# O summed behind the second chunk of V transposes, O and dq packed by ScalarE: decode attention, forward and backward, on one core

## The chip, the cores and the metric

The kernel runs on one core of a Trainium2 chip. The metric is the device time in microseconds (us), the median of several executions. A ratio is the mean time of one kernel's fast runs over the mean of the other's from the same rounds, which is not quite the ratio of the medians quoted beside it.

## The reference

```python
# q, grad_out: [1, 32, 1, 128]; k, v: [1, 32, 8192, 128]; all bfloat16
scores = einsum('bhqd,bhkd->bhqk', q, k) * 128 ** -0.5
attn = softmax(scores)
out_0 = einsum('bhqk,bhkd->bhqd', attn, v)          # O
# out_1, out_2, out_3 = dq, dk, dv by the vector-Jacobian product with grad_out
```

For one query row a head, dk and dv are outer products (ds times q, p times dO), as large as K and V. The kernel reads 134 MB and writes 134 MB.

## The kernel before

Each head loads K and V (2 MB each), and stores dk and dv (2 MB each, in two halves of 1 MB). TensorE transposes V in four chunks, computes the scores of V (dO·V) from them, and sums O and dq over 64 tiles each with one weight load and one matmul of one column per tile. VectorE makes dk and dv. All transfers are issued in order from one queue.

```python
    def v_transposes(h, c):                       # 8 fp32 transposes, one ScalarE copy
        T_ps = psT.tile([P, CH // 2, P], F32, tag="T", name="T_ps")      # two buffers
        for i in range(CH // 2):
            nc.tensor.transpose(T_ps[:, i, :], words[:, m * P:(m + 1) * P], ident_f[:])
        nc.scalar.copy(X[:], T_ps[:])
    def v_scores(h, c):                           # 16 weight loads, 16 matmuls of 2 columns
        ...
    def contract(Xt, rep, out_col, first=0, last=NT):   # a sum: 64 weight loads, 64 matmuls
        for n in range(first, last):
            nc.tensor.matmul(out_col, lhsT=Xt[:, n, :], rhs=rep[:, n, 0:1],
                             start=(n == 0), stop=(n == NT - 1), skip_group_check=True)
    for h in range(H + 1):
        ...  # transposes of K on VectorE, scores of K; dk and dq of the head before; p
        v_transposes(h, 0)
        contract(Vt[h], x["p"], x["m"][:, 2:3])                     # the sum of O
        nc.scalar.copy(o_all[:, h:h + 1], x["m"][:, 2:3])
        v_transposes(h, 1)
        nc.tensor.matmul(x["m"][:, 1:2], lhsT=do_f[...], rhs=o_all[:, h:h + 1], ...)  # dO.O
        v_scores(h, 0)
        v_transposes(h, 2)
        v_scores(h, 1)
        v_transposes(h, 3)
        v_scores(h, 2)
        v_scores(h, 3)
        ...  # dv, its stores, the load of V of head h + 2
    # then, in no fixed order: pack O and dq with VectorE, transpose, store (8 KB each)
```

## Time and profile before

| | before |
|---|---|
| median of 3 runs | 656.67 us (656.61 to 656.91) |
| profiled span | 656.6 us, of a run that took 658.36 us |
| busy: TensorE matmul, VectorE, ScalarE | 79%, 78%, 28% |
| main transfer queue, share of 16 DMA engines | 97.5% |

The share of the transfer queue is an average over 16 engines. Near 100% it says that bytes bound the kernel, but an average cannot show one engine that is slower than the rest, and that engine ends the run. Two means were needed beside the views: the completion records (each transfer counts a semaphore up by 16, and the time of each count is in the trace) and the packet records (start, length and size of each packet, without the engine's number).

### The profile page before, as it was taken

Reading aid. Unit: us, or ns where it says so; the run is one execution under the profiler, and the core shown is the slowest. Engines: PE = TensorE matmul, PEld = TensorE weight load, DVE = VectorE, ACT = ScalarE, POOL = GpSimd, SP = SyncE. Lnnn points to the kernel's source line nnn. Section 1 sums busy time; section 2 is a strip of 40 time slices with the busy share of each in tenths; the row PEclk is TensorE's granted clock in tenths of the full one; section 3 lists DMA queues with packets and bytes.
Section 4 is the critical chain, followed back from the end, with each engine's and each line's share of the span. In section 5 each row is a group of like instructions: output and inputs, shape, how many; then the busy total and the mean of one; then the engine's idle time right before and its main releaser. Section 6 shows DMA issues by size and latency. Waiting matters only on the chain.

```text
span 656.6 us, 21096 instructions
## 1 busy us (share of the span) xinstructions
PE 520.1 (79%) x9705; PEld 485.8 (74%) x9705; DVE 513.8 (78%) x664; ACT 182.2 (28%) x321; POOL 0.7 (0%) x6
## 2 busy tenths in 40 slices
PE   2889788798888777788777887787877888777881
PEld 1888788688888667787777877787866778777881
DVE  5789789788897978778877779777787777887753
ACT  0332223223333122332222322223322233222330
POOL 0000000000000000000000000000000000000000
PEclk9955556656565666655556556666556555555555
DMA  8999999999999999999999999999999999999883
GB/s 334 408 389 428 424 422 430 420 423 430 424 424 428 425 428 423 428 424 427 428 424 426 428 424 425 428 428 423 428 425 424 431 421 426 419 418 412 374 339 149
DMA packets 29368, 269.82 MB, mean 411 GB/s; under 512 B 3424, under 2 KB 3424, under 8 KB 5472
## 3 DMA queue, kind: packets, MB, share of 16 engines
q1 hardware_dynamic: 29280, 268.48, 97.5%
q8 instruction: 76, 1.25, 0.7%
q14 instruction: 12, 0.10, 0.0%
HBM read 134.23 MB, written 134.23 MB: 409 GB/s over the span
## 4 chain that ended last, share of the span: by engine, by line
DMA 63%; PE 23%; DVE 8%; ACT 2%; issue 1%; SPq 0%; ACTq 0%; DVEq 0%
DMA Kt<-in_k_dram 35%; DMA out_dram<-G_dv 29%; PE T_ps L180 10%; DVE XK_sb L142 6%; PE s_ps L154 3%; PE dp_ps L197 2%; PE m_ps L197 2%; PE dp_ps L192 2%; ACT XT_sb L182 1%; PE m_ps L265 1%; PE m_ps L278 1%; DVE G_dk L207 1%; ACT e L277 1%; ACT qd L223 1%; PE s_ps L170 1%
## 5 line engine op out<-in xcount | busy, mean ns | idle before, releaser
L180 PE MATMUL T_ps<-ident_f,Vt 128*128 128x128 f32 x1024 | 237.8, 410 | 0.0
L180 PEld LDWEIGHTS T_ps<-ident_f,Vt 128*128 128x128 f32 x1024 | 198.8, 222 | 0.0
L142 DVE STREAM_TRANSPOSE XK_sb<-Kt 128x1024 f32<-128x1024 f32 x128 | 148.1, 1213 | 63.8 <-DMA Kt<-in_k_dram 63.7
L182 ACT COPY XT_sb<-T_ps 128x1024 f32<-128x1024 f32 x128 | 129.6, 1012 | 160.2 <-PE T_ps L180 160.2
L207 DVE TENSOR_TENSOR G_dv<-p_rep,qd 128x2048 bf16<-128x2048 bf16 x128 | 148.2, 1220 | 14.0 <-DMA out_dram<-G_dv 10.7
L207 DVE TENSOR_TENSOR G_dk<-ds_rep,qd 128x2048 bf16<-128x2048 bf16 x128 | 155.7, 1218 | 1.1
L192 PEld LDWEIGHTS <-XT_sb 128*128 128x128 bf16 x2048 | 77.5, 107 | 30.2 <-ACT XT_sb L182 27.1
L154 PE MATMUL s_ps<-q_blk,XK_sb 128*128 128x4 bf16 x2048 | 59.3, 168 | 44.4 <-DVE pdt L228 41.6
L192 PE MATMUL dp_ps<-do_blk,XT_sb 128*128 128x2 bf16 x2048 | 73.8, 166 | 24.3 <-ACT XT_sb L182 24.3
L154 PEld LDWEIGHTS <-XK_sb 128*128 128x128 bf16 x2048 | 56.8, 103 | 46.3 <-DVE pdt L228 43.4
L197 PE MATMUL dp_ps<-ds_rep,Kt 128*128 128x1 bf16 x2048 | 64.4, 165 | 2.8 <-issue 2.3
L197 PEld LDWEIGHTS <-Kt 128*128 128x128 bf16 x2048 | 59.8, 104 | 8.3 <-issue 8.3
L197 PEld LDWEIGHTS <-Vt 128*128 128x128 bf16 x2048 | 62.6, 105 | 2.0
L197 PE MATMUL m_ps<-p_rep,Vt 128*128 128x1 bf16 x2048 | 60.5, 166 | 0.0
L238 ACT COPY dq_all<-dp_ps 128x1 f32<-128x1 f32 x32 | 5.1, 159 | 191.2 <-PE dp_ps L197 191.2
L278 PEld LDWEIGHTS m_ps<-rs,ones_f 128*128 128x128 f32 x64 | 16.0, 311 | 48.6 <-ACT e L277 48.6
L278 PE MATMUL m_ps<-rs,ones_f 128*128 128x1 f32 x64 | 18.7, 362 | 39.2 <-ACT e L277 39.2
L265 PE MATMUL m_ps<-diag,ones_f 128*128 128x128 f32 x64 | 25.6, 500 | 2.3 <-issue 1.7
L230 DVE SCALAR_TENSOR_TENSOR ds_rep<-dp_ps,pdt,p_s 128x256 bf16<-128x256 f32 x32 | 15.5, 484 | 15.1 <-PE dp_ps L192 12.8
L274 DVE TENSOR_REDUCE nbias<-m_ps 128x1 f32<-128x128 f32 x32 | 9.3, 292 | 20.7 <-ACT qd L223 20.7
L287 ACT ACTIVATE p_rep<-e,rinv 128x256 bf16<-128x256 f32 x32 | 16.2, 508 | 30.3 <-DVE rinv L285 30.3
L223 ACT CAST qd<-m_ps 128x256 bf16<-128x256 f32 x32 | 11.9, 372 | 45.2 <-PE m_ps L219 45.2
(44 smaller groups left out, 161.5 us busy)
## 6 DMA issues: line engine op xcount, KB each, us to landing
Kt<-in_k_dram SPq DMA_DIRECT2D x31, 2048.0 KB, 27.7
Vt<-in_v_dram SPq DMA_DIRECT2D x31, 2048.0 KB, 27.4
out_dram<-G_dv SPq DMA_DIRECT2D x62, 1024.0 KB, 25.3
out_dram<-G_dk SPq DMA_DIRECT2D x62, 1024.0 KB, 25.3
Kt<-in_k_dram SPq DMA_DIRECT2D x4, 512.0 KB, 5.1
Vt<-in_v_dram SPq DMA_DIRECT2D x4, 512.0 KB, 8.2
out_dram<-G_dv SPq DMA_DIRECT2D x4, 512.0 KB, 13.2
out_dram<-G_dk SPq DMA_DIRECT2D x4, 512.0 KB, 9.7
```

Of the source, the lines that this page charges most:

```text
L142: nc.vector.transpose(XK[h][:, :, :, u, :], slots(Kt[h], u, NCH).rearrange("p g d -> p (g d)").bitcast(F32).rearrange("p (g w j) -> p g w ...
L154: nc.tensor.matmul(out[:, g, :], lhsT=cols[:, g, c // 2, c % 2], rhs=q_blk[:, h, c, :], start=(c == 0), stop=(c == 2 * NB - 1), skip_group ...
L180: nc.tensor.transpose(T_ps[:, i, :], words[:, m * P:(m + 1) * P], ident_f[:])
L182: nc.scalar.copy(X[:], T_ps[:])
L192: nc.tensor.matmul(st[h]["dp"][:, n:n + 2], lhsT=X[:, i, e2, :], rhs=do_blk[:, h, e2, :], start=(e2 == 0), stop=(e2 == 1), skip_group_chec ...
L197: nc.tensor.matmul(out_col, lhsT=Xt[:, n, :], rhs=rep[:, n, 0:1], start=(n == 0), stop=(n == NT - 1), skip_group_check=True)
L207: nc.vector.tensor_tensor(slots(G, r, 4).rearrange("p n (a b) -> p n a b", b=R), slots(rep, r, 4).unsqueeze(2).to_broadcast([P, Q, D // R, ...
L223: nc.scalar.copy(x["qd"][:].rearrange("p a d -> p (a d)"), x["m"][:, 256:512])
L230: nc.vector.scalar_tensor_tensor(out=x["ds"][:], in0=x["dp"][:, 0:NT].unsqueeze(2).to_broadcast([P, NT, R]), scalar=pdt[:], in1=x["p_s"][: ...
L265: nc.tensor.matmul(x["m"][:, 128:256], lhsT=ones_f[:], rhs=diag[:], start=True, stop=True, skip_group_check=True)
L278: nc.tensor.matmul(x["m"][:, 0:1], lhsT=ones_f[:], rhs=rs[:], start=True, stop=True, skip_group_check=True)
L287: nc.scalar.activation(x["p"][:], e[:].unsqueeze(2).to_broadcast([P, NT, R]), ACT.Copy, scale=rinv[:])
```

## The change

The intent: let TensorE do the second chunk of transposes before the sum of O, so that it has work while p is made, and do the product behind the third; and take the packing of O and dq off VectorE, where the cast of O stood in front of dv in the last head.

```diff
+    def result(src, dst):
+        half = small.tile([P, H], BF16, tag="half", name="half")
+        nc.scalar.copy(half[:], src[:])
+        fin_ps = psT.tile([P, CH, P], BF16, tag="T", name="fin_ps")
+        nc.tensor.transpose(fin_ps[0:H, 0, :], half[:], ident[:])
+        fin_sb = small.tile([H, D], BF16, tag="fin", name="fin_sb")
+        nc.scalar.copy(fin_sb[:], fin_ps[0:H, 0, :])
+        nc.sync.dma_start(dst.rearrange("b h s d -> (b h s) d"), fin_sb[:])
@@
         v_transposes(h, 0)
+        v_transposes(h, 1)
         contract(Vt[h], x["p"], x["m"][:, 2:3])
         nc.scalar.copy(o_all[:, h:h + 1], x["m"][:, 2:3])
-        v_transposes(h, 1)
+        v_scores(h, 0)
+        v_transposes(h, 2)
         nc.tensor.matmul(x["m"][:, 1:2], lhsT=do_f[:, h:h + 1].to_broadcast([P, P]), rhs=o_all[:, h:h + 1],
                          start=True, stop=True, skip_group_check=True)
-        v_scores(h, 0)
-        v_transposes(h, 2)
         v_scores(h, 1)
@@
+        if h == H - 1:
+            result(o_all, out_0)
+    result(dq_all, out_1)
     order.__exit__(None, None, None)
-    for src, dst in ((o_all, out_0), (dq_all, out_1)):
-        ...  # the same with nc.vector.tensor_copy in place of nc.scalar.copy
```

More of the change, by code (lines that the diff above doesn't have):

```diff
@@ L307 @@
         outer(h, "dv", 3)
+        if h == H - 1:
+            result(o_all, out_0)
+    result(dq_all, out_1)
     order.__exit__(None, None, None)
-    for src, dst in ((o_all, out_0), (dq_all, out_1)):
-        half = small.tile([P, H], BF16, tag="half")
-        nc.vector.tensor_copy(half[:], src[:])
-        fin_ps = psT.tile([P, CH, P], BF16, tag="T")
-        nc.tensor.transpose(fin_ps[0:H, 0, :], half[:], ident[:])
-        fin_sb = small.tile([H, D], BF16, tag="fin")
-        nc.vector.tensor_copy(fin_sb[:], fin_ps[0:H, 0, :])
-        nc.sync.dma_start(dst.rearrange("b h s d -> (b h s) d"), fin_sb[:])
 _INS = ['q', 'k', 'v', 'grad_out']
```

## The prediction

> **What bounds the kernel now.** I read the page first, for the busy shares and the slices.
>
> ```profile
> PE 520.1 (79%) x9705; PEld 485.8 (74%) x9705; DVE 513.8 (78%) x664; ACT 182.2 (28%) x321; POOL 0.7 (0%) x6
> ...
> DMA  8999999999999999999999999999999999999883
> GB/s 334 408 389 428 424 422 430 420 423 430 424 424 428 425 428 423 428 424 427 428 424 426 428 424 425 428 428 423 428 425 424 431 421 426 419 418 412 374 339 149
> ...
> q1 hardware_dynamic: 29280, 268.48, 97.5%
> ```
>
> No compute engine is over 79%, while the 16 DMA engines are busy 97.5% of the whole span and hold 418 to 431 GB/s from the fourth slice to the 36th. Between those slices the change can do nothing unless it moves bytes or starves the queue, and it does neither. Only the ends (16.4 us a slice) are left: the last three slices fall to 374, 339 and 149 GB/s, which looks as if computing set the pace there. So I cut the end into stretches:
>
> ```profile
> core 0: us, PE busy (x) PEld busy (x) DVE busy (x) ACT busy (x) POOL busy (x), PEclk, DMA share, GB/s
> ...
> 120.00:600.00 480.00, 390.45 (x7306) 365.15 (x7304) 382.49 (x481) 136.67 (x241) 0.00 (x0) 0.55 1.01 425
> ...
> 640.00:643.00 3.00, 2.05 (x72) 1.91 (x69) 2.72 (x3) 0.16 (x1) 0.00 (x0) 0.50 0.22 82
> 643.00:648.00 5.00, 0.29 (x1) 0.10 (x1) 2.70 (x5) 0.00 (x0) 0.00 (x0) 0.50 0.96 384
> 648.00:649.00 1.00, 0.00 (x0) 0.00 (x0) 0.00 (x0) 0.00 (x0) 0.00 (x0) 0.50 0.47 155
> 649.00:655.00 6.00, 0.00 (x0) 0.00 (x0) 0.00 (x0) 0.00 (x0) 0.00 (x0) 0.50 0.06 25
> 655.00:656.60 1.60, 0.00 (x0) 0.00 (x0) 0.00 (x0) 0.00 (x0) 0.00 (x0) 0.50 0.00 0
> ```
>
> The row 649 to 655 decides the case. Every compute engine is done, and the DMA share is 0.06, which is one engine in sixteen (1/16 = 0.0625), moving 25 GB/s. The packet records there show 4096-byte packets, one at a time, 155 ns from start to start without a gap until 654.9: one DMA engine working off a backlog, about 6 us behind the other fifteen.
>
> The completion records tell how long it has been behind. Each transfer counts its semaphore up by 16, and I compared the 16th count with the 15th: 2.0 us later at 89 us, 2.0 at 192, 4.9 at 404, 7.2 at 645, 5.9 at 652. The laggard is late in nearly every transfer after the first 25 us, and its lag mostly grows. Its own landings at the end have no hole: 634.76, 637.38, 639.99, 642.79, 645.34 (1 MB transfers, 2.5 to 2.8 apart), then 646.58, 647.81, 649.06, 650.33 (the last dv, 512 KB), 651.55, 652.78, 654.01, 655.23 (the last dk), 655.43 and 655.62 (the two small results).
>
> What it must move accounts for most of the span. Its share is one sixteenth of everything: 62 loads of 8 packets of 16 KB at about 0.607 us from start to start (301 us), 124 stores of 8 packets of 8 KB at 0.305 (303), and 16 transfers of 8 packets of 4 KB at 0.155 (20), in all 624 us from 2.1 us on. An undisturbed engine would end near 626; this one takes 29 us longer, part of it instruction fetches (76 packets of 16 KB in the other queue, shared out among several engines in a way that I can't see). The time is thus 655.6, when the most loaded DMA engine ends, plus 1.0 to close.
>
> **What the Trainium skill says.** (1) "DMA: Bandwidth & Descriptors", "Why a DMA increments its semaphore by 16 and not by 1": a transfer runs on up to 16 engines that finish independently, and only the full count means that all landed. The trace agrees: 5.9 us between 15th and 16th count at the end. (2) Same page, "Where 436 GB/s comes from": the ports carry 435.2 GB/s; the trace holds 425 from 120 to 600 us, 98% of it. (3) "TensorE: Matmul & The Clock Gate", "Architectural detail: the array is 16× 32×32, not 1× 128×128": ScalarE and VectorE execute strictly in order. The trace agrees, at the one place where before pays for it:
>
> ```profile
> 628.80 0.51 ACT L287 ACTIVATE p_rep<-e,rinv 128x256 bf16<-128x256 f32 x1 [0.94 <-DVE rinv L285]
> ...
> 632.02 0.16 ACT L292 COPY o_all<-m_ps 128x1 f32<-128x1 f32 x1 [0.67 <-PE m_ps L197]
> 632.22 0.18 DVE L313 CAST half<-o_all 128x32 bf16<-128x32 f32 x1 [3.15 <-ACT o_all L292]
> 632.31 4.63 DVE L207 TENSOR_TENSOR G_dv<-p_rep,qd 128x2048 bf16<-128x2048 bf16 x4
> ...
> 639.62 0.50 PEld L192 LDWEIGHTS <-XT_sb 128*128 128x128 bf16 x16 [0.72 <-ACT XT_sb L182]
> 640.25 0.48 DVE L230 SCALAR_TENSOR_TENSOR ds_rep<-dp_ps,pdt,p_s 128x256 bf16<-128x256 f32 x1 [0.92 <-PE dp_ps L192]
> 640.76 4.63 DVE L207 TENSOR_TENSOR G_dk<-ds_rep,qd 128x2048 bf16<-128x2048 bf16 x4
> ```
>
> In the last head the small cast of O stands in front of VectorE's G_dv in the queue and waits 3.15 us for the sum of O, though p_rep was ready at 629.3.
>
> **The change, part by part.** *Order on TensorE, 32 heads.* Before: T0 (8 transposes), sum of O, T1, product dO·O, scores 0, T2, scores 1, T3, scores 2, 3. After: T0, T1, sum, scores 0, T2, product, scores 1, T3, and so on. What stands before T3 is the same set: three transpose chunks of about 1.81 us, a sum of 1.68, a product of 0.22, scores of 0.43 and 0.40. It would gain if TensorE stood still for p_rep before the sum or for the copy of O before the product. It doesn't: groups of the sum show 0.0 us idle, and in the last head the product follows T1 directly (632.02 is the copy's start, 633.59 the product's). So 0 of 32 heads gain; the order only widens margins (p_rep was ready 0.8 us before the sum). It frees the V buffer with T3 at the same moment.
>
> *O and dq by ScalarE.* Off VectorE: 2 casts (0.18 and 0.17 us) and 2 copies (0.21 each), 0.77 us of 513.8; with the first cast goes its 3.15 us wait. On ScalarE the same four cost about 0.16 to 0.25 each, by its 128x1 copy of 0.16: under 1 us on an engine at 28%. G_dv of the last head should start near 629.3, three us earlier, and its four stores issue near 630.5, 631.7, 632.9 and 634.8 (the last waits for its semaphore's earlier transfer, landed 634.76) in place of 633.55 to 636.96. ds_rep still hangs on scores 3, which hang on the copy of T3: 640.2 again, so G_dk stays at 640.8 to 645.4.
>
> *Stores of O and dq.* O's 8 KB store moves from behind the last dk stores (issued 646.60) to before them (near 641); dq's keeps the end. On the laggard that exchanges a 0.2 us piece with later pieces.
>
> Sum on the path that sets the end: bytes 0, packets 0, the laggard's start 0. Three us earlier G_dv is worth nothing: its first store was issued at 633.55 and the laggard reached it only after 645.34. The sum is 0.0 us, and I allow a few tenths either way.
>
> **Rivals.** *The tail is computing.* The chain of waits ends in DVE and PE (scores 3, ds_rep, G_dk, fin_sb), with no DMA after 616.9. If that chain set the end, removing 3.15 us in front of G_dv, and the late packing of O, would give 1 to 4 us: 653 to 655.5. Against it: the chain stops at 646 and the end comes 10 us later; the first dk store was issued at 642.02, when the laggard still had work until 650.33, so G_dk has 8 us of slack.
>
> *A new wait.* Transfers issue in order from one queue, and the eight semaphores are used in turn: dq's store went at 647.9, just after the transfer eight before it landed at 647.81. O's store moved forward shifts the dk stores by one: the third goes when 645.34 has landed and not at 644.29, the fourth after 646.58 and not at 645.42. If the laggard were not backed up, this would cost about 1.2 us: 657.8. It has work until 653 then, so I expect 0. Likewise O's packing on ScalarE comes behind the copy of T3 and its transpose behind scores 3; near 0.3 us of TensorE before dq's sum, which again only the 8 us of slack would see.
>
> *The laggard's own luck.* Fetches and slow packets (around 33 to 38 us some 16 KB packets took 1 to 2 us) could fall differently when TensorE's order changes. Three runs within 0.30 us speak for a repeatable pattern, but a new program may have another: perhaps 1 us either way. This sets most of my range.
>
> **Range and chances.** Centre 656.6, as before. Down to 655.2 if there is a little in the tail or a luckier laggard; up to 658.0 for the semaphore shift or an unlucky one. Two per cent is 13.1 us; no part comes near it. Faster over 2%: 0.01; within: 0.98; slower: 0.01.
>
> **What would show it.** G_dv of the last head starting at 629 to 630 with its wait gone; no VectorE cast of O; ds_rep within 0.5 us of 640.3 against the start; stretches of one engine (0.06) at the end again, longer than 6 us since the other fifteen finish dv earlier; the last landing near 655.6; about 425 GB/s from 120 to 600. I am wrong if that one-engine stretch shrinks and the end moves with G_dk, or if the middle falls below 420 GB/s.

## The result, and the profile after

The changed kernel took 651.34 us (650.3 to 651.95, 4 runs) where before took 656.78 (656.61 to 656.91, 4 runs): ratio 0.9916, 95% interval 0.9898 to 0.9933. This is within 2%, as forecast, but 5.4 us faster and below the range's lower end of 655.2.

The page of the changed kernel, shares and slices:

```profile
PE 501.7 (77%) x9705; PEld 469.2 (72%) x9705; DVE 513.7 (79%) x660; ACT 183.2 (28%) x325; POOL 0.7 (0%) x6
...
GB/s 328 418 411 425 423 423 426 421 426 426 424 428 427 424 428 427 424 426 429 425 424 428 425 426 428 424 427 428 422 427 426 425 428 427 423 430 423 422 357 223
...
q1 hardware_dynamic: 29280, 268.48, 98.3%
```

Packets and bytes are the same, and so is the middle; only the last slices are fuller (223 in place of 149 GB/s). The stretches of its end, with the columns of those shown of before:

```profile
120.00:600.00 480.00, 379.41 (x7326) 354.77 (x7323) 385.68 (x486) 136.36 (x243) 0.00 (x0) 0.57 1.01 426
...
643.00:645.00 2.00, 0.00 (x0) 0.00 (x0) 0.00 (x0) 0.00 (x0) 0.00 (x0) 0.50 0.21 85
645.00:647.00 2.00, 0.00 (x0) 0.00 (x0) 0.00 (x0) 0.00 (x0) 0.00 (x0) 0.50 0.06 25
647.00:648.50 1.50, 0.00 (x0) 0.00 (x0) 0.00 (x0) 0.00 (x0) 0.00 (x0) 0.50 0.00 0
```

There is still a stretch of one engine (0.06), but it is 2 us long and not 6. The completion records say the same: the last transfer's 16th count comes at 647.57, 2.0 after the 15th (before: 655.62, 5.95 after). The bandwidth from 120 to 600 us is 426 against 425 GB/s, no visible difference, because the loss was on one engine of sixteen: 5.8 us in 480 is 1.2% of a sixteenth.

The timeline of the last head shows most of what the prediction said of the engines (G_dv and G_dk are the tiles in which dv and dk are made, from p_rep and ds_rep):

```profile
620.81 0.51 ACT L296 ACTIVATE p_rep<-e,rinv 128x256 bf16<-128x256 f32 x1 [0.94 <-DVE rinv L294]
621.63 4.63 DVE L207 TENSOR_TENSOR G_dv<-p_rep,qd 128x2048 bf16<-128x2048 bf16 x4 [0.55 <-DMA out_dram<-G_dv]
...
630.08 0.22 ACT L242 CAST half<-o_all 128x32 bf16<-128x32 f32 x1
...
630.86 0.48 DVE L230 SCALAR_TENSOR_TENSOR ds_rep<-dp_ps,pdt,p_s 128x256 bf16<-128x256 f32 x1 [3.81 <-PE dp_ps L192]
...
631.38 4.63 DVE L207 TENSOR_TENSOR G_dk<-ds_rep,qd 128x2048 bf16<-128x2048 bf16 x4
```

The cast of O no longer stands before G_dv, which starts 0.3 us after p_rep is done. Yet ds_rep waits longer for TensorE (3.81 us in place of 0.92), as it hangs on the last scores. The whole head lies 9.4 us earlier than before (ds_rep at 630.86, was 640.25), so the time was won long before the tail.

Where it was won: I added up, transfer by transfer, how much longer the slowest engine took between two of its landings than its packets' ordinary lengths give (16 KB 0.607 us from start to start, 8 KB 0.305, 4 KB 0.155). In the 13th to 42nd transfer the profiled run of the changed kernel loses 1.0 us less, in the next 128 (some 130 to 560 us) 5.8 less, in the rest 1.2 less: the 8.0 us between the two last landings. (The two profiled runs took 658.36 and 650.30 us, so they lie further apart than the medians, which differ by 5.4.) In those 128 transfers it is one transfer of each head that differs. The landing of the first half of dk takes 0.33 us too long before and 0.07 after, in the mean over the heads; each of the other five differs by less than 0.06.

The packets of that transfer can be followed. The records do not name the engine, but on one engine a packet starts 3 to 13 ns before the one in front of it has ended, and its 8 packets a transfer and its semaphore write must come where the 16th count is; this picks one chain out of the 16, back to the eleventh transfer. It is an inference, and in a few places may have slipped to another engine. A check needs no chain: of the 1,647 store packets of all engines that lie by more than half in before's sums of O between 60 and 620 us, 79 took 340 to 480 ns, no two of these at once, and 76 of them are of the chain; the 1,540 others off the chain are 0.1 ns over 309 in the mean. So it is one engine at a time, and nearly always the one picked. For one head (start in us, length in ns, bytes; the last column is what TensorE was doing, from the timeline):

```
before: end of the store of the first half of dk   after: the same store
265.32  331  8192   transposes of V            262.02  322  8192   transposes of V
265.65  318  8192   transposes, then sum of O  262.34  320  8192   transposes of V
265.96  329  8192   sum of O                   262.65  318  8192   transposes of V
266.28  380  8192   sum of O                   262.97  311  8192   transposes of V
266.65  389  8192   sum of O                   263.27  321  8192   transposes of V
267.02  380  8192   sum of O                   263.59  309  8192   transposes of V
267.41  653 16384   (load of K)                263.90  613 16384   (load of K)
                                               264.51  616 16384   sum of O, load of K
```

The timelines give the sum of O in these heads, before and after:

```profile
265.90 1.89 PE L197 MATMUL m_ps<-p_rep,Vt 128*128 128x1 bf16 x64
```

```profile
264.30 1.84 PE L197 MATMUL m_ps<-p_rep,Vt 128*128 128x1 bf16 x64
```

Before, the sum ran from 265.90 to 267.79 while the slowest engine stored dk, and its packets grew from 309 to 380 ns. After, the sum starts when this store is over and lies on the load of K, whose packets keep their length: 76 of them in the sum were 6 ns over 611 in the mean. (Before, 29 load packets lay in the sum and were 27 over; in the head shown it is the first behind the store, 653.) From 60 to 620 us, 107 store packets of the slowest engine fell by more than half into the sum of O before, 51.6 ns longer than 309 each, in all 5.5 us; after, it is 12 packets and 0.3 us. That this is repeated in every head I put down to the pace of the head, which that engine sets: VectorE waits for its landing of K.

```profile
DVE XK_sb L142 <- DMA Kt<-in_k_dram: 63.7, 23, 3.6
```

This line of before's waits (total us, times, longest) shows it for 23 of the 32 heads. It fixes the place of each transfer of the slowest engine against each instruction of a head.

### The profile page after: what moved, and what is told of

Read it like the earlier page. It is cut to its first block, busy times and chain, and to the rows that moved or that the text cites. A ratio compares the mean times of both kernels' runs of the same rounds, so it can differ in the third digit from the quotient of the medians.

```text
span 648.5 us, 21097 instructions
## 1 busy us (share of the span) xinstructions
PE 501.7 (77%) x9705; PEld 469.2 (72%) x9705; DVE 513.7 (79%) x660; ACT 183.2 (28%) x325; POOL 0.7 (0%) x6
## 4 chain that ended last, share of the span: by engine, by line
DMA 68%; PE 16%; DVE 11%; ACT 2%; issue 1%; DVEq 0%; SPq 0%; ACTq 0%
DMA Kt<-in_k_dram 38%; DMA out_dram<-G_dv 29%; DVE XK_sb L142 8%; PE T_ps L180 6%; PE s_ps L154 2%; PE dp_ps L197 2%; PE m_ps L197 1%; PE dp_ps L192 1%; ACT XT_sb L182 1%; PE m_ps L274 1%; DVE G_dv L207 1%; DVE G_dk L207 1%; PE m_ps L287 1%; PE s_ps L170 1%; DVE ds_rep L230 0%
## 5 line engine op out<-in xcount | busy, mean ns | idle before, releaser
L180 PE MATMUL T_ps<-ident_f,Vt 128*128 128x128 f32 x1024 | 216.7, 391 | 0.0
L180 PEld LDWEIGHTS T_ps<-ident_f,Vt 128*128 128x128 f32 x1024 | 192.4, 214 | 0.0
L207 DVE TENSOR_TENSOR G_dv<-p_rep,qd 128x2048 bf16<-128x2048 bf16 x128 | 148.2, 1220 | 14.2 <-DMA out_dram<-G_dv 10.9
L154 PE MATMUL s_ps<-q_blk,XK_sb 128*128 128x4 bf16 x2048 | 59.7, 168 | 54.3 <-DVE pdt L228 51.6
L192 PEld LDWEIGHTS <-XT_sb 128*128 128x128 bf16 x2048 | 71.7, 104 | 28.6 <-ACT XT_sb L182 27.1
L197 PEld LDWEIGHTS <-Vt 128*128 128x128 bf16 x2048 | 60.0, 101 | 1.5
L197 PE MATMUL m_ps<-p_rep,Vt 128*128 128x1 bf16 x2048 | 58.6, 165 | 0.0
```

Of the source, the lines that this page charges most:

```text
L154: nc.tensor.matmul(out[:, g, :], lhsT=cols[:, g, c // 2, c % 2], rhs=q_blk[:, h, c, :], start=(c == 0), stop=(c == 2 * NB - 1), skip_group ...
L192: nc.tensor.matmul(st[h]["dp"][:, n:n + 2], lhsT=X[:, i, e2, :], rhs=do_blk[:, h, e2, :], start=(e2 == 0), stop=(e2 == 1), skip_group_chec ...
L207: nc.vector.tensor_tensor(slots(G, r, 4).rearrange("p n (a b) -> p n a b", b=R), slots(rep, r, 4).unsqueeze(2).to_broadcast([P, Q, D // R, ...
```

## The experiments

Theory A: the slowest DMA engine stores slower while TensorE runs the short instructions of the sum; the order takes the sum out of a store. Theory B: the gain is VectorE's wait and the packing at the end. Theory C: luck of where instruction fetches and odd long packets fall. Each run was timed against before on its own chip.

**order_only: before with the new order alone.**

```diff
         v_transposes(h, 0)
+        v_transposes(h, 1)
         contract(Vt[h], x["p"], x["m"][:, 2:3])
         nc.scalar.copy(o_all[:, h:h + 1], x["m"][:, 2:3])
-        v_transposes(h, 1)
-        <product>
         v_scores(h, 0)
         v_transposes(h, 2)
+        <product>
```

> The kernel before with the new order on TensorE alone (sum of O behind the second chunk, product behind the third); the results still packed by VectorE. Theory A (the sum of O, when it runs while the slowest DMA engine stores dk, lengthens that engine's 8 KB packets from 309 to about 370 ns, 5.5 us in all; the order takes it out of that window): all of the gain, 650.3 to 652.2, and the one-engine stretch at the end shrinks to 2 or 3 us. Theory B (the gain is VectorE's freed wait and the packing at the end): 656 to 657. Theory C (luck of where instruction fetches fall): anything from 649 to 657.

Measured: 650.75 us (650.7 to 651.33) against 656.57 of before, ratio 0.9906 (0.9891 to 0.9921), correct. This is all of the gain. Store packets of the slowest engine in the sum: 13, in all 0.3 us; the last 16th count comes 2.2 us after the 15th.

**result_only: the changed kernel with the old order.**

```diff
         v_transposes(h, 0)
-        v_transposes(h, 1)
         contract(Vt[h], x["p"], x["m"][:, 2:3])
         nc.scalar.copy(o_all[:, h:h + 1], x["m"][:, 2:3])
+        v_transposes(h, 1)
+        <product>
         v_scores(h, 0)
         v_transposes(h, 2)
-        <product>
```

> The changed kernel with the old order on TensorE: only the results packed by ScalarE. Theory A: 656.0 to 657.2, as before, though G_dv of the last head starts 3 us earlier. Theory B: 650 to 653. Theory C: anything from 649 to 657.

Measured: 657.39 us (656.6 to 658.22) against 656.57, ratio 1.0005 (0.9988 to 1.0022), correct: nothing. Its timeline of the last head and the stretch of its end:

```profile
627.17 0.51 ACT L296 ACTIVATE p_rep<-e,rinv 128x256 bf16<-128x256 f32 x1 [0.94 <-DVE rinv L294]
627.92 4.63 DVE L207 TENSOR_TENSOR G_dv<-p_rep,qd 128x2048 bf16<-128x2048 bf16 x4 [0.48 <-DMA out_dram<-G_dv]
```

```profile
648.50:653.00 4.50, 0.00 (x0) 0.00 (x0) 0.00 (x0) 0.00 (x0) 0.00 (x0) 0.50 0.06 26
```

The 3.15 us wait before G_dv is gone here too, and bought nothing: one engine (0.06) still works off its backlog to the end. The store packets in the sum are back: 104, 52.2 ns over each. Theory B falls.

**sum_as_transposes and sum_tiny: what it is about the sum.** Both give a wrong O on purpose, in before's order.

```diff
 # sum_as_transposes
-        contract(Vt[h], x["p"], x["m"][:, 2:3])
+        for n in (0, NT - 1):
+            nc.tensor.matmul(x["m"][:, 2:3], lhsT=Vt[h][:, n, :], rhs=x["p"][:, n, 0:1], ...)
+        for n in range(8):
+            nc.tensor.transpose(x["m"][:, 128:256], <fp32 words of V>[:, n * P:(n + 1) * P], ident_f[:])
 # sum_tiny, for 62 of the 64 terms
+                nc.tensor.matmul(x["m"][0:32, 3:4], lhsT=Vt[h][0:32, n, 0:32], rhs=x["p"][0:32, n, 0:1],
+                                 start=True, stop=True, skip_group_check=True)
```

> Wrong results on purpose. Before's order; the sum of O is cut to its first and last term and eight fp32 transposes of V take its time and place (about 1.9 us of TensorE with few, long instructions in place of 128 short ones). Theory A: the collision is gone though nothing else has moved: 649.5 to 652, and on the slowest engine the dk stores at that place take about 320 ns a packet. Rival A2 (what matters is when the second chunk and the scores run, not the sum): 656 to 657, since they run when they did before.

> Wrong results on purpose. Before's order; 62 of the 64 terms of the sum read a 32x32 corner of V in place of 128x128: as many instructions, a sixteenth of the weights' bytes. If it is the rate of TensorE's instructions that slows the engine: 655.5 to 657, packets still near 370 ns there. If it is the bytes that TensorE reads from SBUF: 649.5 to 652, packets near 310 ns.

Measured: sum_as_transposes 647.28 us (647.16 to 647.69), ratio 0.9853 (0.9836 to 0.9869); sum_tiny 658.13 (657.02 to 658.68), ratio 1.0014 (0.9997 to 1.0031); before 656.57. In the first, 110 store packets of the slowest engine fell into the transposes put in the sum's place and were 4.3 ns over, in place of 51.6 (8 ns when the chain was drawn a second time; of all engines' store packets there, none took 340 to 480 ns). In the second, 101 fell into the small sum and were 47.2 ns over, with one sixteenth of the weights' bytes. The groups of sum_tiny show that its small matmuls take almost the time of the full ones (160 and 166 ns):

```profile
L296 PE MATMUL m_ps<-p_rep,Vt 32*32 32x1 bf16 x1984 | 57.8, 160 | 0.0
```

So neither the bytes of the weights nor TensorE's being busy lengthens the packets. What the two sums share, and the transposes don't, is 128 instructions in 1.9 us, 67 a microsecond. That the rate is the cause is argued: the transposes also differ in type (fp32, the sums bf16), and no run separates the two. The time of sum_as_transposes is lower than theory A's range of 649.5 to 652; it also has 17,641 instructions in place of 21,096 and 62 instruction fetches in place of 76, so not all of its gain need belong to the store.

**sum_first and sum_third: the sum at other places.**

```diff
 # sum_first, in before            # sum_third, in after
+        <sum of O>                         v_transposes(h, 1)
         v_transposes(h, 0)        -        <sum of O, copy>
-        <sum of O>                         v_scores(h, 0)
         <copy>                             v_transposes(h, 2)
         v_transposes(h, 1)        -        <product>
                                   +        <sum of O, copy>
                                            v_scores(h, 1)
                                            v_transposes(h, 3)
                                   +        <product>
```

> Before's kernel with the sum of O moved the other way, ahead of the first chunk of transposes, where it has to wait about 1 us for p. In before's clock that is some 12.4 to 14.3 us after the last K transposes begin, and the slowest engine stores the second half of dk from about 12.6 to 15.1. Theory A (what counts is that the 128 short instructions of the sum fall on that store): as before or nearly, 655.5 to 657.5. If the gain of the change came only from giving the second chunk its place, or from the sum being early or late as such: not determined, but there would be no reason to find before's time again.

> The changed kernel with the sum one chunk later still, behind the third chunk (product behind the fourth). Theory A: the slowest engine is loading K from about 15 to 20 us of the head, the sum at about 17 to 19 is inside this load, and loads are not lengthened (in the changed kernel 76 load packets of 16 KB in the sum lost 6 ns each): 649.5 to 652.5, no loss and no further gain. If each step later gives some: 646 to 648.

Measured: sum_first 657.19 us (656.77 to 657.44), ratio 0.9998 (0.9983 to 1.0013), with 132 store packets in the sum, 51.5 ns each. sum_third 649.68 (649.66 to 650.4), ratio 0.9888 (0.9872 to 0.9905), with 15. Both correct, before 657.13. (The store that the expectation calls the second half of dk is the first half.) Two different orders with the sum on the store give before's time, and orders with it on the load of K give 649.7 to 651.3; chance in theory C would not sort itself so. Nor does TensorE's granted clock: sum_first's runs had 0.67 and before's time, order_only's 0.58 to 0.59 and all of the gain.

**s3_late and s23_late: scores of V moved.** After the change the largest remaining loss of this kind was in the scores of V, 114 store packets at 30 ns.

```diff
             k_scores(h)
         if h > 0:
+            v_scores(p_, 2)          # s23_late only
+            v_scores(p_, 3)
             ds_of(p_)
@@
-        v_scores(h, 2)               # s23_late only
-        v_scores(h, 3)
```

> The changed kernel with the last 32 short instructions of the scores of V behind the scores of K of the next head. In the changed kernel the store packets of the slowest engine that fall in the scores of V lose 30 ns each (114 packets, 3.4 us), most in the last two groups. There the engine should be loading V. Theory A: 1 to 2 us less, 648.5 to 650.5, unless the later ds on VectorE (about 2 us later in each head) takes up the 2.7 us that VectorE stands idle for K. Rival: VectorE becomes the bound: 652 to 665.

> The same with the last two groups (64 short instructions) behind the scores of K. Theory A: 1.5 to 3 us less than the changed kernel, 647.5 to 650. Rival: ds comes about 3 us later and takes up all of VectorE's idle time for K: 652 to 675.

Measured: 656.25 us (655.96 to 656.92), ratio 0.9986 (0.9971 to 1.0001), and 658.75 (657.77 to 659.54), ratio 1.0022 (1.0007 to 1.0037), before 657.13; both correct. Both expectations of a gain failed, and both times lie in the range given for the rival that VectorE becomes the bound (652 to 665 and 652 to 675), so the time alone does not decide. The waits of s3_late speak against it:

```profile
DVE ds_rep L230 <- PE dp_ps L192: 76.3, 32, 4.1
...
DVE XK_sb L142 <- DMA Kt<-in_k_dram: 18.6, 19, 1.9
```

It still waits for K, though less. In s23_late this wait is down to

```profile
DVE XK_sb L142 <- DMA Kt<-in_k_dram: 7.8, 10, 2.1
```

so in 22 of 32 heads K was there in time, VectorE waits for the scores instead (89.3 us in all before ds_rep), and computing is near to setting the pace. But both kernels still end on one backlogged engine: the last 16th count comes 5.1 us (s3_late) and 4.3 us (s23_late) after the 15th. What happened in s3_late is that ds, and with it the sums of dq, came later and left the load of V for the store of dv behind it: 92 store packets of the slowest engine lie in the sums of dq, 40.6 ns each, 3.7 us, where the changed kernel has 13 and 0.2 us, and 1.4 us come in the scores of K (0.3). I had moved one burst and forgotten what hangs on it.

**sum_fourth and after_again: the sum last.**

```diff
         v_transposes(h, 1)
-        <sum of O, copy>
         v_scores(h, 0)
         v_transposes(h, 2)
-        <product>
         v_scores(h, 1)
         v_transposes(h, 3)
+        <sum of O, copy>
         v_scores(h, 2)
         v_scores(h, 3)
+        <product>
```

> The changed kernel with the sum of O behind the fourth chunk of transposes, the product last. The sum then runs while ScalarE copies the fourth chunk, a wait of 0.8 us in each head before, so that the last scores end about 0.8 us earlier and the sum and all four groups of scores should lie inside the slowest engine's load of K. Theory A: its store packets in the scores of V (114, 30 ns each in the changed kernel) mostly come back to 309 ns: 1.5 to 3.5 us less than the changed kernel, 647.5 to 650 where the changed kernel takes 651. If only the sum mattered: equal to the changed kernel or to the version with the sum third, 649.7 to 652.

> The changed kernel itself, on the same chip as the run beside it, for a comparison on one chip: 650 to 652 if before takes 656 to 657.

Measured on one chip: sum_fourth 650.80 us (650.4 to 651.43), ratio 0.9906 (0.9889 to 0.9923); the changed kernel 650.69 (650.33 to 651.0), ratio 0.9903 (0.9888 to 0.9918); before 656.89; both correct. The expected further gain did not come. The scores still have 71 store packets at 37 ns (45 when the chain was drawn a second time), and the product, now behind them, 30 at 38.5. My explanation, which no run tests: the store of the second half of dk begins when the last packet of K has gone, some 0.4 us before the landing that VectorE sees, so 0.8 us earlier was not early enough.

**k_after_v: move the transfer and not the instructions.**

```diff
-        if 0 < h and h + 2 < H:
-            load_k(h + 2)            # was behind the first half of dk
@@
             load_v(h + 2)
+        if 0 < h and h + 2 < H:
+            load_k(h + 2)
```

> The changed kernel with the load of K issued behind the load of V, so that each DMA engine gets V, K, dv, dk, dk, dv in place of K, dk, dv, V, dv, dk. TensorE's order is not touched. Then the scores of K and the sums of dq (192 short instructions and more, 5 to 9 us after the K landing), which in the changed kernel lie on the load of V, should lie on stores of the slowest engine. Theory A (stores are lengthened, loads not; which transfer is under way decides): about 12 packets a head at 40 to 60 ns, 0.5 us in some 25 heads, so 8 to 15 us slower than the changed kernel: 658 to 666, with some 300 store packets of the slowest engine in the scores of K and the sums of dq. Rival (only the place of TensorE's instructions counts, or the effect belongs to the sum of O alone): 650 to 652. If K comes too late for the next head, VectorE waits for it more than 2.7 us a head and the time is over 666 without such packets.

Measured: 671.54 us (668.95 to 673.56), ratio 1.0207 (1.0173 to 1.0242), before 657.21, correct: slower, though not clearly by 2%. The packets are as theory A said: 153 store packets of the slowest engine in the scores of K at 48.2 ns and 150 in the sums of dq at 56.8, 15.9 us together (after: 25 packets, 0.5 us), and 80 load packets in the sum of O at 1.1 ns. TensorE's order is the changed kernel's, so for the packets it is the pairing of burst and store that counts, and the sum of O is nothing special. The time says less. It lies above the range of 658 to 666, where the expectation had put a late K: VectorE's wait for K did rise, from 65.0 us in all to 101.1, and the middle (120 to 600 us) fell from 426 to 412 GB/s with more than one engine slowed: of 291 load packets of 640 to 900 ns between 60 and 620 us only 17 are of the slowest engine's chain (after: 26 and 3). Two more losses are in it: load packets beside the transposes took 8.8 us too long, a few of them very long (median 1 ns), which I can't explain, and the end is no longer backlogged, since the last six transfers, from O's result to dq's, land on the slowest engine within 0.7 us of the 15th count (663.05 to 670.12).

The runs, with the store packets of the slowest engine between 60 and 620 us that lie by more than half in the sum of O (in sum_as_transposes, in what stands in its place). The three rows marked * and the second figures of sum_fourth are from a chain drawn a second time; for the other rows it gives the last column within 0.4 us:

| kernel | median us | packets in the sum, mean ns over 309 | total us over 309, all its stores |
|---|---|---|---|
| before | 656.78 | 107, 51.6 | 14.3 |
| result_only | 657.39 | 104, 52.2 | 14.5 |
| sum_tiny | 658.13 | 101, 47.2 | 14.5 |
| sum_first | 657.19 | 132, 51.5 | 15.7 |
| s3_late | 656.25 | 39, 28.2 | 14.5 |
| s23_late | 658.75 | 56, 30.6 | 14.2 |
| k_after_v * | 671.54 | 0 | 19.4 |
| after | 651.34 | 12, 25.8 | 9.6 |
| after_again * | 650.69 | 17, 7.3 | 9.5 |
| order_only | 650.75 | 13, 26.0 | 9.8 |
| sum_third | 649.68 | 15, 23.6 | 8.9 |
| sum_fourth | 650.80 | 37, 19.4 or 31.1 | 7.8 or 9.1 |
| sum_as_transposes * | 647.28 | 106, 8.1 | 7.2 |

Without k_after_v and sum_as_transposes, which stand at the two ends in both columns, the last column sorts the kernels into two groups, 14.2 to 15.7 us and 7.8 to 9.8, and the times fall into the same two: 656.3 to 658.8 and 649.7 to 651.3. sum_third has the lowest time of the correct kernels, but its interval overlaps that of the changed kernel, so it isn't shown to be better.

## Why the prediction was right or wrong

**The bound was right.** One DMA engine, behind the others, ended the run before and after. The last stretch of 0.06 is there in both.

**The tail was right.** G_dv of the last head starts as p_rep is done, the cast of O is off VectorE, ds_rep hangs on the last scores; result_only shows that the 3 us were worth 0 (1.0005). The new wait through the shifted semaphores was hidden, as said: in the changed kernel dq's store was issued at 639.97, and the slowest engine had work until 647.

**TensorE's order was right as far as TensorE goes.** No head gains a standstill; the gain did not come from there.

**The step that failed** is "Sum on the path that sets the end: bytes 0, packets 0, the laggard's start 0", and ahead of it "Between those slices the change can do nothing unless it moves bytes or starves the queue, and it does neither". Both took the length of a packet as given, 305 ns from start to start. The runs showed that it isn't: on the slowest engine, store packets grow by about 50 ns while TensorE runs a burst of short instructions, and a change that adds no byte and frees no wait can move such a burst off a store. That was worth 5.5 us before, 0.3 after. The trace of before held it: I saw the lag grow with every head, and explained the 29 us by fetches and luck without asking which transfer lost the time. Half of them, 14.3 us, were lengthened stores. The growth per transfer, sorted by its place in the head, would have shown one store at about 0.33 us in each head.

**The luck term was mis-sized and misnamed.** "A new program may have another: perhaps 1 us either way" was about the right mechanism's place, the lengths of the laggard's packets, but it was no luck: order_only, after and after_again agree within 0.7 us, and so do result_only, sum_first and before.

**One sum agreed by chance.** The prediction took 655.6 plus 1.0 to close for the time and found before's median. But 656.6 is the span of a run that took 658.36 us; the runs of the median, 656.67, had shorter spans. Nothing rested on it.

**My own test was right.** "I am wrong if that one-engine stretch shrinks" is what happened: 6 to 2 us.

**What stays open.** Why one engine alone is sensitive: before, some 1,330 store packets of all sixteen lay wholly within the sum from 60 to 600 us (those over 480 ns left out) and lost 5.4 us together, no more than the slowest engine's own. What in a dense run of TensorE instructions reaches it (their fetches, their semaphores, or the recording of the profile itself; every timed run here lists a span and a granted clock, so none is known to be free of recording) is not settled. Also open is the part of the gain that is not in the sum: of the 8.0 us between the two profiled runs, 5.2 are the sum's, of which the other stores took 0.5 back (14.3 to 9.6 in all); the loads of that engine lost 3.4 us less (7.3 to 4.0 over 611 ns in the whole run). Part of that is the run and not the kernel, since before's profiled run was 1.6 us over its median and the loads lost 5.7 in result_only and 4.1 in sum_first. In time, 1.0 falls in the first transfers (from 30 to 41 us, 22 packets of all engines took over 1 us before and 3 after), the rest is not traced.

## What to carry to other kernels

When a kernel is bound by transfers, look for the engine that ends last, take its excess per transfer and sort it by the transfer's place in the loop: one place that loses the same every time points to something that runs beside it. An order of instructions on a compute engine that isn't the bound can then still be worth something, because it decides which transfer lies beside which burst; here sums and scores of many short matmuls belong beside loads and not beside stores. And before such a burst is moved, follow what hangs on it, since the next burst moves too.

## What the Trainium skill lacked or had wrong

- "DMA: Bandwidth & Descriptors", "Latency and other measured facts", says that engines 7 and 15 are usually slower, and puts it down, as a best guess, to the descriptor rings of the path from GpSimd; the path from SP, it says, has no such ring. Here all transfers are issued from SP and one engine is still slower, 5.9 us behind the 15th at the end before and 2.0 after. Which engine it is the records don't say.
- "SBUF — State Buffer", "SBUF: two separate sides", says that a DMA cannot be slowed by a compute op. Here stores are slowed while TensorE runs short instructions, though this does not show where: packets of 8 KB went from 309 to about 360 ns (mean 51.6 over) on one DMA engine beside 67 instructions a microsecond, with full weights (before) and with a sixteenth of them (47.2 over), and only 4.3 over beside fp32 transposes. Whether a run without the profiler's recording shows it too is open.
- "Runtime: NRT & Kernel Launch", "Instruction fetch mechanics", says that instructions are fetched in blocks of 16 KiB, 256 instructions. The trace agrees: 76 packets of 16,384 bytes for 19,410 instructions of TensorE (75.8 blocks). It calls the cost mostly hidden; in a kernel bound by transfers each packet takes a DMA engine's time (the record of one spans 0.94 us in the median, 0.7% of the 16 engines' span for all), which the page doesn't mention.
